# Low parts of weight blocks on VectorE, two blocks converted later, weight tiles in turned order, scaling on ScalarE: one change in four pieces

## The chip, the cores and the metric

The program runs on one core of one Trainium2 chip. The core has TensorE (matrix products, which only write the PSUM), VectorE, ScalarE and GpSimd (element by element; in the profile DVE, ACT and POOL) and SyncE (SP), which issues the DMAs here. Every engine runs its own list of instructions in order and waits at semaphores for the others. The metric is the time of one execution on the device in microseconds.

## The reference

Three parts follow each other, all in f32. The first is attention over 4 sequences of 576 tokens with 8 heads of 64 columns, with a mask by blocks of 64 tokens:

```python
scores = np.where(block_i >= block_j, scale * q @ k.T, -1e9)
attn = np.exp(scores - scores.max(-1)); attn /= attn.sum(-1) + 1e-9
x = attn @ v                                  # 2304 tokens x 512
h = x @ w_in                                  # 512 -> 2048
x = (h - np.tanh(h)) @ w_out                  # 2048 -> 512
xn = x / np.sqrt(np.mean(x * x, -1) + 1e-6) * rms_g
g = xn @ w_gate                               # 512 -> 1536
out = (g / (1 + np.exp(-g)) * (xn @ w_val)) @ w_out2
```

The five weight matrices arrive as 64-bit floats; the kernel turns their bits into f32 itself.

## The kernel before, in words

A product of two f32 matrices is made of three products with operands rounded to the shorter type f32r: each operand is split into a high part (`rnd`, line 100, mostly on ScalarE) and a low part, the difference between the full value and the high part (`lo`, line 105). So wherever TensorE needs a new operand, a rounding on ScalarE and a difference on VectorE or GpSimd come first. In the matmul lines 683 to 685, 873 to 875 and 961 to 963 the three belong together.

**First stage.** Tokens stand in 6 groups of 384. A step `s` is one of 16 blocks of 128 columns of the first feed-forward part in one group (`g, j = divmod(s, J1)`): 12 matmuls make `h`, ScalarE takes the tanh (line 881), VectorE the difference (line 887), ScalarE rounds it to `gh`, VectorE makes `gl`, and a step later 9 matmuls in `out1` add it into the sums of the group. Attention for the following groups is interleaved at slots of the step (`aslot`). In it `scores` takes the maximum on VectorE (line 479) and the exponential on ScalarE (line 481); after three tiles the reciprocal of the sums (line 490) and three scalings of the probabilities (line 494), which stood on GpSimd for the first two units and on VectorE for the later ones; `transp` turns the tiles on TensorE (line 507), and `av` multiplies by the values. The weights are converted in group 0, written to DRAM, and loaded again in every later group, two tiles of 512 KB in each step, into a ring of four (`w1get`).

**Blocks for the last part.** The last part uses a scheme with seven products instead of eight over pairs of token groups, so each of its 12 blocks of gate and value weights, and six of the output weights, becomes seven blocks of 256 columns. `Convert` does this: `load` (DMA), `piece` twice (lines 137 to 142 in `convert`), `sums` on GpSimd (four operations, lines 729 to 733), and the split into high part (ScalarE, line 738) and low part (line 739), in two halves of three and four column blocks. The list `away` does that in groups 2 to 4 for the output blocks and those gate blocks that are not in `DIRECT`, and writes them to DRAM. The blocks in `DIRECT` are made in place, in group 5 and while the first pair runs, and `keep` writes them out for the pairs behind.

**Last part.** For each of 3 pairs of groups `p` there are 12 steps `fast` of 42 matmuls (lines 961 to 963), with adds on VectorE (lines 1008 to 1018), Silu on ScalarE and a product on GpSimd (line 1017); behind them `tail` multiplies by the output weights, `sums(j)` (GpSimd, line 1024) having prepared further operands. Weights lie in three slots that `load_slot` fills two steps ahead.

TensorE's order is the order of the program text. The instructions of the other engines are put in order by a scheduler ahead of the run, except those in `pin`, which keep their order among themselves; so a change in one place can change the order of an engine elsewhere.

Of the kernel before, what the change touches and what calls it, by code (L numbers as in the profile page):

```python
# [10 lines left out]
F32 = mybir.dt.float32  # L11
# [40 lines left out]
DIRECT = (0, 1, 2, 3, 4, 6, 8)  # L52
# [39 lines left out]
def build(ctx, tc, q, k, v, w_in, w_out, w_gate, w_val, w_out2, rms_g, ident_in, out):  # L92
# [256 lines left out]
    class Attn:  # L349
# [107 lines left out]
        def scores(self, i, u, ti, d):  # L457
# [118 lines left out]
    with tc.manual_schedule(engines={PE.engine}):  # L576
# [20 lines left out]
        def jof(s):  # L597
            g, j = divmod(s, J1)
            return j
# [7 lines left out]
        def until(s):  # L607
            return s
# [102 lines left out]
        class Convert:  # L711
# [12 lines left out]
            def sums(self):  # L724

                f = self.f.rearrange("p g (k c) -> p (g k) c", k=2)
                o = self.o = env["cvp"].tile([128, 4, 256], F32, name="fs", tag="fs")
                gate = self.kind == "g"
                POOL.tensor_tensor(out=o[:, 0], in0=f[:, 3], in1=f[:, 2], op=ALU.add if gate else ALU.subtract)
                POOL.tensor_tensor(out=o[:, 2], in0=f[:, 1], in1=f[:, 3], op=ALU.subtract)  # L730
                x, y = (o[:, 0], f[:, 1]) if gate else (f[:, 1], o[:, 0])
                POOL.tensor_tensor(out=o[:, 1], in0=x, in1=y, op=ALU.subtract)
                POOL.tensor_tensor(out=o[:, 3], in0=f[:, 0], in1=o[:, 1], op=ALU.subtract)
# [7 lines left out]
            def split(self, w, eng):  # L741
                self.split_part(w[:, :, 0:3], eng, 0)
                self.split_part(w[:, :, 3:7], eng, 1)
                self.w = w

# [3 lines left out]
            def send(self, eng, half):  # L749
# [3 lines left out]
                self.split_part(w, eng, half)  # L753
# [6 lines left out]
        def away(units, eng):  # L760

            items = []
            for n, c in enumerate(units):
# [10 lines left out]
                def third(c=c):  # L774
                    c.sums()
                    c.send(eng, 0)
                items += [first, second, third, lambda c=c: c.send(eng, 1)]
# [42 lines left out]
        def slot(q):  # L820
# [4 lines left out]
                     + [Convert("g", j) for j in range(J2) if j not in DIRECT], POOL)  # L825
# [12 lines left out]
        for s in range(NSA):  # L838
# [61 lines left out]
            if 2 <= g < NG - 1:  # L900
                nit = {2: 0, 3: 10, 4: 26}[g] + (j + 1) * {2: 10, 3: 16, 4: 24}[g] // J1
                while 44 - len(items) < min(nit, 44):
                    items.pop(0)()
            if j == J1 - 1:
                while att.pos < goal:
                    att.step()
                if g == NG - 2:
# [20 lines left out]
                    items = away([direct[j] for j in DIRECT[:5]], POOL)  # L928
                    for n in range(3):
                        items[4 * n + 2] = direct[n].sums  # L930
                        items[4 * n + 3] = lambda n=n: direct[n].split(slot(n), POOL)
# [36 lines left out]
        BLOCK = {1: 2, 2: 0, 3: 1, 4: 6, 5: 3, 6: 4, 7: 5}  # L968

        KEEP = {0: 1, 1: 2, 2: 3, 3: 4, 5: 6, 7: 8}  # L970

        def load_slot(q):
# [4 lines left out]
            if j < J2:  # L977
                if p == 0 and j in direct:
                    direct[j].split(w, DVE)
# [6 lines left out]
        def temp(name, dt=F32):  # L986
            return w2b.tile([128, TG], dt, name=name, tag=name, bufs=2)
# [6 lines left out]
        def fast(s, j, x):  # L994
# [20 lines left out]
            DVE.tensor_tensor(c12, prod(6, xc, 1), c12, ALU.add)  # L1015
# [18 lines left out]
        def tail(p):  # L1034
# [19 lines left out]
            a = [temp(n)[:, 0:256] for n in ("c11", "c11", "c12")]  # L1054
# [71 lines left out]
        for p in range(NG // 2):  # L1126
            for j in range(J2):
# [4 lines left out]
                if p == 0:  # L1132
                    if j + 3 in direct:
                        if j + 3 >= 5:
                            direct[j + 3].piece(1)
                        direct[j + 3].sums()
# [34 lines left out]
```

## Time and profile before

| | |
|---|---|
| median of 3 runs | 1094.34 us (1094.28 to 1095.1) |
| the profiled execution | 1095.53 us, span 1093.7 us |
| TensorE busy | 1039.3 us, 95% of the span |
| VectorE busy | 844.5 us, 77% |
| ScalarE busy | 602.4 us, 55% |
| GpSimd busy | 442.6 us, 40% |
| granted clock of TensorE, mean | 0.981 |
| DMA | 291.74 MB, 267 GB/s |

The span runs from the first to the last instruction; the execution's own time has 1.8 us around it. A share over the whole span mixes stages, so the table by stages in the rows below is of more use. Group 2 begins near 250 us, group 5 near 580 us, the first pair of the last part at 674 us, its tail near 761 us.

### The profile page before, as it was taken

What the parts mean: (1) busy time and instruction counts of PE and PEld (TensorE: products, weight loads), DVE (VectorE), ACT (ScalarE), POOL (GpSimd) and SP (SyncE); (2) the same over time, 40 slices, a digit from 0 to 9 for tenths busy, and PEclk for the clock granted to TensorE, in tenths of its full rate; (3) what the DMA queues carried; (4) which work ended last, traced back from release to release, by engine and by line L of the source; (5) the groups of instructions that cost most, each with busy time, mean ns of one, the idle gap of its engine ahead of it and who ended that gap; (6) DMA issues with size and microseconds to landing.
All of it is one profiled execution on the core that took longest, in us unless ns stands there. A gap on an engine that the chain in (4) does not pass through costs nothing.

```text
span 1093.7 us, 18315 instructions
## 1 busy us (share of the span) xinstructions
PE 1039.3 (95%) x6020; PEld 943.4 (86%) x6020; DVE 844.5 (77%) x1714; ACT 602.4 (55%) x1390; POOL 442.6 (40%) x529
## 2 busy tenths in 40 slices
PE   7799999998899999999799899999999999999998
PEld 5566669997889988889688798999999998999998
DVE  5888867787878988888885677988886688866776
ACT  5877757667667776766665456442632226422253
POOL 5531111123434446445555564457421275212550
PEclk9999999999889999999999899999999999999999
DMA  9788888988779999997878996986687665786664
GB/s 224 231 282 293 271 282 269 275 237 247 201 185 255 263 330 290 319 298 244 282 253 299 371 355 215 391 311 253 238 282 286 252 246 198 277 296 248 233 224 162
DMA packets 192815, 291.74 MB, mean 267 GB/s; under 512 B 109776, under 2 KB 151120, under 8 KB 185424
## 3 DMA queue, kind: packets, MB, share of 16 engines
q1 hardware_dynamic: 192720, 290.57, 81.6%
q8 instruction: 48, 0.79, 0.3%
q14 instruction: 47, 0.39, 0.1%
HBM read 227.08 MB, written 63.44 MB: 266 GB/s over the span
## 4 chain that ended last, share of the span: by engine, by line
PE 71%; DVE 12%; ACT 6%; DMA 5%; issue 4%; POOL 1%; SPq 1%; DVEq 0%; ACTq 0%; POOLq 0%
PE gv L961 8%; PE gv L963 8%; PE gv L962 8%; PE gv L685 4%; PE t L873 4%; PE gv L684 4%; PE gv L683 4%; PE t L874 4%; PE t L875 4%; PE acc L685 3%; PE acc L683 3%; PE t L466 3%; PE acc L684 3%; PE acc L693 3%; PE t L560 2%
## 5 line engine op out<-in xcount | busy, mean ns | idle before, releaser
L961 PE MATMUL gv<-xh,ws 128*128 128x384 f32 x504 | 169.0, 335 | 1.0 <-DVE x2s L102 1.0
L963 PE MATMUL gv<-xh,ws 128*128 128x384 f32 x504 | 169.2, 336 | 0.0
L962 PE MATMUL gv<-xl,ws 128*128 128x384 f32 x504 | 169.0, 335 | 0.0
L873 PE MATMUL t<-xh,w 128*128 128x384 f32 x384 | 139.5, 363 | 0.1
L874 PE MATMUL t<-xl,w 128*128 128x384 f32 x384 | 130.6, 340 | 1.1 <-POOL xl L105 1.1
L875 PE MATMUL t<-xh,w 128*128 128x384 f32 x384 | 130.5, 340 | 0.0
L685 PE MATMUL acc<-w,gl 128*128 128x512 f32 x240 | 99.2, 413 | 12.8 <-DVE gl L105 12.8
L1017 POOL TENSOR_TENSOR g<-c,c 128x384 f32<-128x384 f32 x36 | 40.5, 1124 | 165.9 <-ACT c L1016 160.1
L683 PE MATMUL acc<-w,gh 128*128 128x512 f32 x240 | 101.3, 422 | 2.4 <-ACT gh L100 2.4
L481 ACT ACTIVATE pt<-pt,stat 128x64 f32<-128x64 f32 (+2 forms) x144 | 80.3, 559 | 42.0 <-DVE pt L479 41.2
L1014 ACT ACTIVATE gt<-c 128x384 f32<-128x384 f32 x36 | 18.9, 525 | 144.0 <-DVE c L1013 144.0
L684 PE MATMUL acc<-w,gh 128*128 128x512 f32 x240 | 97.1, 405 | 0.0
L961 PEld LDWEIGHTS gv<-xh,ws 128*128 128x128 f32 x504 | 94.6, 188 | 1.4 <-ACT sq L701 1.4
L963 PEld LDWEIGHTS gv<-xh,ws 128*128 128x128 f32 x504 | 94.6, 188 | 0.0
L962 PEld LDWEIGHTS gv<-xl,ws 128*128 128x128 f32 x504 | 94.6, 188 | 0.0
L873 PEld LDWEIGHTS t<-xh,w 128*128 128x128 f32 x384 | 73.5, 191 | 4.4 <-issue 0.7
L874 PEld LDWEIGHTS t<-xl,w 128*128 128x128 f32 x384 | 73.5, 191 | 3.5 <-POOL xl L105 1.4
L100 ACT ACTIVATE pp<-t 128x512 fp32r<-128x512 f32 (+6 forms) x152 | 64.1, 438 | 16.9 <-PE t L507 16.4
L479 DVE TENSOR_SCALAR_CACHE_REDUCE pt<-t 128x64 f32<-128x64 f32 (+2 forms) x144 | 63.7, 448 | 12.2 <-PE t L466 11.2
L875 PEld LDWEIGHTS t<-xh,w 128*128 128x128 f32 x384 | 72.9, 190 | 0.0
L105 DVE TENSOR_TENSOR gl<-gt,gh 128x384 fp32r<-128x384 f32 x80 | 60.8, 761 | 15.0 <-ACT gh L100 14.8
L887 DVE TENSOR_TENSOR gt<-t,gt 128x384 f32<-128x384 f32 x80 | 44.0, 550 | 35.6 <-ACT gt L881 35.5
(168 smaller groups left out, 2935.4 us busy)
## 6 DMA issues: line engine op xcount, KB each, us to landing
ws<-w2d SPq DMA_DIRECT2D x29, 1792.0 KB, 7.5
w<-w1d_i SPq DMA_DIRECT2D x80, 512.0 KB, 5.6
w<-w1d_o SPq DMA_DIRECT2D x64, 512.0 KB, 5.5
ws<-wod SPq DMA_DIRECT2D x21, 1536.0 KB, 6.1
st<-in_moe_w_out SPq DMA_DIRECT2D x28, 512.0 KB, 4.7
w2d<-ws SPq DMA_DIRECT2D x7, 1792.0 KB, 11.6
st<-in_moe_w_in SPq DMA_DIRECT2D x16, 512.0 KB, 5.4
w1d_i<-w SPq DMA_DIRECT2D x16, 512.0 KB, 4.6
```

What stands on the lines that cost most here:

```text
L100: ACT.activation(out=o, in_=i, func=AF.Copy)
L479: DVE.tensor_scalar(pt[:, a:z], s[:, 0:z - a], -0.125, least, ALU.mult, ALU.min, accum_out=mx)
L481: ACT.activation(out=pt[:, 0:keys], in_=pt[:, 0:keys], func=AF.Exp, scale=-1.0, bias=least, accum_out=st[:, 8 + ti:9 + ti])
L683: PE.matmul(acc, lhsT=gh[:, c], rhs=wh, start=first, stop=False)
L684: PE.matmul(acc, lhsT=gh[:, c], rhs=wl, start=False, stop=False)
L685: PE.matmul(acc, lhsT=gl[:, c], rhs=wh, start=False, stop=last)
L873: PE.matmul(h, lhsT=wh[:, c], rhs=xh[:, kk], start=(kk == 0), stop=False)
L874: PE.matmul(h, lhsT=wh[:, c], rhs=xl[:, kk], start=False, stop=False)
L875: PE.matmul(h, lhsT=wl[:, c], rhs=xh[:, kk], start=False, stop=(kk == KD - 1))
L961: PE.matmul(ps, lhsT=wh[:, c], rhs=xh[:, kk], start=(kk == 0), stop=False)
L962: PE.matmul(ps, lhsT=wh[:, c], rhs=xl[:, kk], start=False, stop=False)
L963: PE.matmul(ps, lhsT=wl[:, c], rhs=xh[:, kk], start=False, stop=(kk == nk - 1))
```

## The change

Four pieces. (1) The low parts of all converted blocks are made on VectorE instead of GpSimd; the four sums are now written over their inputs, so the first half is split before the sums and the second behind them (`fill`). The order of the seven products in `fast` follows, and two adds that read the same product become one of 768 columns. (2) Blocks 9 and 10 join `DIRECT`: they are no longer converted in groups 2 to 4, but while the first pair runs; their staging space is freed two steps later, so `sums` of the first pair start at step 9. (3) In groups 3 and 5 the weight tiles are taken from last to first, and the four that a group ends with are used by the next one without loading. (4) The scalings of the probabilities of the later units go from VectorE to ScalarE.

```diff
-DIRECT = (0, 1, 2, 3, 4, 6, 8)
+DIRECT = (0, 1, 2, 3, 4, 6, 8, 9, 10)
...
-                (POOL if u.light else DVE).tensor_scalar(pv, pv, st[:, 16 + t:17 + t], 1.0, ALU.mult, ALU.mult)
+                if u.light:
+                    POOL.tensor_scalar(pv, pv, st[:, 16 + t:17 + t], 1.0, ALU.mult, ALU.mult)
+                else:
+                    ACT.activation(out=pv, in_=pv, func=AF.Copy, scale=st[:, 16 + t:17 + t])
...
         def jof(s):
             g, j = divmod(s, J1)
-            return j
+            return J1 - 1 - j if back(g) else j
+
+        def back(g):
+            return g > 2 and g % 2 == 1
...
         def until(s):
-            return s
+            g, j = divmod(s, J1)
+            return s + 2 * (J1 - 1 - j) + 1 if 2 <= g < NG - 1 and j >= J1 - 4 else s
...
-                o = self.o = env["cvp"].tile([128, 4, 256], F32, name="fs", tag="fs")
...
-                POOL.tensor_tensor(out=o[:, 2], in0=f[:, 1], in1=f[:, 3], op=ALU.subtract)
+                POOL.tensor_tensor(out=f[:, 3], in0=f[:, 1], in1=f[:, 3], op=ALU.subtract)
...
-            def split_part(self, w, eng, half):
+            def split_part(self, w, half):
...
-                x = self.o if half else self.f.rearrange("p g (k c) -> p (g k) c", k=2)[:, 0:3]
+                x = self.f.rearrange("p g (k c) -> p (g k) c", k=2)[:, 0:4 if half else 3]
                 pin(ACT.activation(out=w[:, 0], in_=x, func=AF.Copy))
-                eng.tensor_tensor(out=w[:, 1], in0=x, in1=w[:, 0].bitcast(F32), op=ALU.subtract)
+                lo(DVE, w[:, 1], x, w[:, 0])
...
+            def fill(self, w, half):
                 self.w = w
+                self.split_part(w[:, :, 3:7] if half else w[:, :, 0:3], half)
+                if not half:
+                    self.sums()
...
-                nit = {2: 0, 3: 10, 4: 26}[g] + (j + 1) * {2: 10, 3: 16, 4: 24}[g] // J1
-                while 44 - len(items) < min(nit, 44):
+                nit = {2: 0, 3: 8, 4: 20}[g] + (j + 1) * {2: 8, 3: 12, 4: 20}[g] // J1
+                while 36 - len(items) < min(nit, 36):
...
-            DVE.tensor_tensor(c22, ps, c12, ALU.add)
-            DVE.tensor_tensor(c21, ps, c21, ALU.add)
+            ps = prod(6, xc, 0).rearrange("p (o c) -> p o c", o=1).broadcast_to([128, 2, TG])
+            DVE.tensor_tensor(vb, ps, va, ALU.add)
...
-                if p == 0 and j == JH:
+                if p == 0 and j == 8:
                     sw0.close()
                     sums_pool = sw.enter_context(tc.tile_pool(name="sums", bufs=1, side="right"))
-                if j > JH:
-                    if j == JH + 1:
-                        sums(0)
+                if j > 8:
+                    if j == 9:
+                        for k in range(3):
+                            sums(k)
                     sums(j - JH)
```

Line numbers move: the new lines 735 to 739 are the sums of a block (729 to 733 before), 744 its high part (738), 888 the tanh (881), 1019 to 1029 the adds and the last product of a step (1008 to 1019), 1027 GpSimd's product (1017), 1034 `sums` (1024), 801 and 803 the scaling and the differences of `xn` (794 and 796).

On GpSimd before, in the first pair, from the product of step 8 (`g1_8`) to that of step 10, each step's product is followed by three sums (`gs`) and then by the four differences of `xn`:

```order
L1017 TENSOR_TENSOR g1_8_8693<-c12_8638,c22_8640 128x384
L1024 TENSOR_TENSOR gs2_0_8705<-g1_2_8207,g1_8_8693 128x384
L1024 TENSOR_TENSOR g1_2_8207<-g0_2_8217,g1_2_8207 128x384
L1024 TENSOR_TENSOR gs2_1_8706<-gs2_0_8705,g0_2_8217 128x384
L1017 TENSOR_TENSOR g1_9_8768<-c12_8713,c22_8715 128x384
L1024 TENSOR_TENSOR gs3_0_8786<-g1_3_8290,g1_9_8768 128x384
L1024 TENSOR_TENSOR g1_3_8290<-g0_3_8300,g1_3_8290 128x384
L1024 TENSOR_TENSOR gs3_1_8787<-gs3_0_8786,g0_3_8300 128x384
L796 TENSOR_TENSOR xn_8543<-xn_8543 128x256 x4
L1017 TENSOR_TENSOR g1_10_8849<-c12_8794,c22_8796 128x384
```

On GpSimd now, the same place; `fu_8358` is block 10:

```order
L1027 TENSOR_TENSOR g1_8_8585<-va_8532,vb_8533 128x384
L735 TENSOR_TENSOR fu_8358<-fu_8358 128x256
L736 TENSOR_TENSOR fu_8358<-fu_8358 128x256
L1027 TENSOR_TENSOR g1_9_8659<-va_8606,vb_8607 128x384
L738 TENSOR_TENSOR fu_8358<-fu_8358 128x256
L739 TENSOR_TENSOR fu_8358<-fu_8358 128x256
L803 TENSOR_TENSOR xn_8432<-xn_8432 128x256 x4
L1034 TENSOR_TENSOR gs0_0_8677<-g1_0_7911,g1_6_8420 128x384
L1034 TENSOR_TENSOR gs1_0_8682<-g1_1_7987,g1_7_8506 128x384
L1034 TENSOR_TENSOR gs2_0_8687<-g1_2_8075,g1_8_8585 128x384
L1034 TENSOR_TENSOR gs3_0_8692<-g1_3_8151,g1_9_8659 128x384
L1034 TENSOR_TENSOR g1_0_7911<-g0_0_7921,g1_0_7911 128x384
```

The sums of block 10 stand on both sides of the product of step 9, and twelve `gs` sums (five are shown up to here) come in one run. They end with `gs3_1`, and the products of steps 10 and 11 follow, still on GpSimd now:

```order
L1034 TENSOR_TENSOR gs3_1_8693<-gs3_0_8692,g0_3_8161 128x384
L1027 TENSOR_TENSOR g1_10_8753<-va_8700,vb_8701 128x384
L803 TENSOR_TENSOR xn_8518<-xn_8518 128x256 x2
L1034 TENSOR_TENSOR gs4_0_8771<-g1_4_8238,g1_10_8753 128x384
L803 TENSOR_TENSOR xn_8518<-xn_8518 128x256
L1034 TENSOR_TENSOR g1_4_8238<-g0_4_8248,g1_4_8238 128x384
L1034 TENSOR_TENSOR gs4_1_8772<-gs4_0_8771,g0_4_8248 128x384
L1027 TENSOR_TENSOR g1_11_8832<-va_8779,vb_8780 128x384
```

The products of steps 10 and 11, which the tail reads, have moved behind the sums of the earlier steps. On VectorE now, between the last operations of step 9 and the first of step 10:

```order
L1028 TENSOR_TENSOR vb_8607<-gv_8661,vb_8607 128x384
L1029 TENSOR_TENSOR g0_9_8669<-vb_8607,gt_8608 128x384
L801 SCALAR_TENSOR_TENSOR xn_8432<-xn_8432,rinv_119,g_bc_7040 128x512
L801 SCALAR_TENSOR_TENSOR xn_8432<-xn_8432,rinv_119,g_bc_7040 128x2x256
L105 TENSOR_TENSOR gl_8878<-g1_9_8659,gh_8877 128x384
L105 TENSOR_TENSOR ws_8521<-fu_8358,ws_8521 128x1024
L1019 TENSOR_TENSOR va_8700<-gv_8711,c11_8699 128x384
```

The low part of block 10's second half (`ws`, 1024 columns) has come in between step 9's scaling of `xn` and step 10's first add; there was no such instruction here before. In the first stage, a unit of attention in group 3, VectorE before has the scalings between the low part of one step and the difference of the next:

```order
L105 TENSOR_TENSOR gl_4910<-gt_4906,gh_4909 128x384
L490 RECIPROCAL stat_4766<-stat_4766 128x3
L494 TENSOR_SCALAR pt_4767<-pt_4767,stat_4766 128x448
L494 TENSOR_SCALAR pt_4767<-pt_4767,stat_4766 128x512
L494 TENSOR_SCALAR pt_4767<-pt_4767,stat_4766 128x576
L140 TENSOR_SCALAR cv_4943<-cv_4943 128x512
L105 TENSOR_TENSOR pp_4892<-t_4965,pp_4892 128x8x64
L887 TENSOR_TENSOR gt_4978<-t_4958,gt_4978 128x384
```

ScalarE now has them (line 497) at this place, between the tanh and the rounding to `gh`:

```order
L489 ACTIVATE stat_4719<-stat_4719 128x3
L100 ACTIVATE pp_4851<-t_4922 128x8x64
L888 ACTIVATE gt_4935<-t_4915 128x384
L497 ACTIVATE pt_4720<-pt_4720,stat_4719 128x448
L497 ACTIVATE pt_4720<-pt_4720,stat_4719 128x512
L497 ACTIVATE pt_4720<-pt_4720,stat_4719 128x576
L100 ACTIVATE pp_4851<-t_4942 128x8x64
L100 ACTIVATE pp_4851<-t_4949 128x2x64
L100 ACTIVATE gh_4938<-gt_4935 128x384
```

The three scalings stand between the same step's tanh (`gt_4935`) and rounding (`gh_4938`) and moved from one engine's list to the other's.

## Rows read from the trace of the kernel before

**Rows 1.** Busy time by stages: start:end, us, engines, clock, DMA share, GB/s.

```profile
250.00:350.00 100.00, 90.56 (x496) 82.47 (x495) 81.14 (x207) 69.20 (x184) 38.71 (x55) 0.91 0.78 219
350.00:455.00 105.00, 100.23 (x545) 89.19 (x543) 91.47 (x192) 72.92 (x166) 50.19 (x57) 1.00 1.01 291
455.00:580.00 125.00, 115.96 (x619) 103.93 (x620) 97.71 (x192) 83.21 (x181) 65.77 (x74) 0.96 0.87 280
580.00:674.00 94.00, 87.30 (x437) 76.84 (x435) 64.34 (x93) 51.95 (x98) 53.26 (x46) 0.96 0.85 301
674.00:761.00 87.00, 86.55 (x496) 86.58 (x497) 74.28 (x124) 35.75 (x65) 46.05 (x45) 1.00 0.89 335
761.00:808.00 47.00, 44.57 (x369) 44.01 (x369) 41.65 (x70) 25.77 (x54) 23.35 (x23) 1.00 0.66 239
```

**Rows 2.** TensorE's waits, 170 to 690 us: waiter, releaser, us, times, longest.

```profile
PE acc L685 <- DVE gl L105: 12.8, 10, 3.4
...
PE t L531 <- DVE pp L105: 2.7, 3, 1.2
PE acc L683 <- ACT gh L100: 2.4, 1, 2.4
PE t L466 <- DVE avt L534: 2.1, 1, 2.1
PE t L507 <- DVE pt L479: 2.0, 1, 2.0
```

**Rows 3.** VectorE's timeline near 427 and 600 us: start, duration, instruction, idle before.

```profile
427.34 2.85 DVE L141 SCALAR_TENSOR_TENSOR cv<-cv,cu 128x512 int32<-128x512 int32 x1
...
597.78 2.23 DVE L140 TENSOR_SCALAR cv<-cv 128x512 f32<-128x512 f32 x1 [2.13 <-ACT cv L137]
600.12 0.69 DVE L141 SCALAR_TENSOR_TENSOR cv<-cv,cu 128x512 int32<-128x512 int32 x1
600.73 0.42 DVE L140 TENSOR_SCALAR cv<-cv 128x512 f32<-128x512 f32 x1
```

**Rows 4.** GpSimd's timeline at the same two places.

```profile
427.27 2.37 POOL L739 TENSOR_TENSOR wc<-fs,wc 128x1024 fp32r<-128x1024 f32 x1 [1.89 <-ACT wc L738]
...
597.33 2.41 POOL L739 TENSOR_TENSOR wc<-fs,wc 128x1024 fp32r<-128x1024 f32 x1 [5.27 <-ACT wc L738]
```

**Rows 5.** TensorE's timeline behind the first of them.

```profile
430.71 0.50 PE L685 MATMUL acc<-w,gl 128*128 128x512 f32 x1 [2.29 <-DVE gl L105]
```

**Rows 6.** Groups by line and form, low parts: count, busy us, mean ns, idle before.

```profile
L739 POOL TENSOR_TENSOR wc<-fs,wc 128x1024 fp32r<-128x1024 f32 x11 | 26.5, 2413 | 15.4 <-ACT wc L738 12.8 <-issue 1.8 <-POOL xs L535 0.7
...
L739 DVE TENSOR_TENSOR ws<-fs,ws 128x1024 fp32r<-128x1024 f32 x4 | 4.9, 1222 | 1.8 <-ACT ws L738 1.8
```

**Rows 7.** Groups by line: the scalings on VectorE, the exponentials on ScalarE.

```profile
L494 DVE TENSOR_SCALAR pt<-pt,stat 128x64 f32<-128x64 f32 (+5 forms) x96 | 40.8, 480 | 0.2
...
L481 ACT ACTIVATE pt<-pt,stat 128x64 f32<-128x64 f32 (+2 forms) x144 | 80.3, 559 | 42.0 <-DVE pt L479 41.2
```

**Rows 8.** Groups by line and form, operations of the last part.

```profile
L1012 DVE TENSOR_TENSOR c<-gv,c 128x384 f32<-128x384 f32 x36 | 19.7, 548 | 0.0
...
L794 DVE SCALAR_TENSOR_TENSOR xn<-xn,rinv,g_bc 128x512 f32<-128x512 f32 x18 | 19.7, 1133 | 0.0
...
L1016 ACT ACTIVATE c<-c 128x384 f32<-128x384 f32 x36 | 18.9, 525 | 14.1 <-DVE c L1015 14.1
...
L738 ACT ACTIVATE ws<-fs 128x1024 fp32r<-128x1024 f32 x7 | 7.4, 1059 | 6.8 <-POOL fs L733 6.7
...
L1017 POOL TENSOR_TENSOR g<-c,c 128x384 f32<-128x384 f32 x36 | 40.5, 1124 | 165.9 <-ACT c L1016 160.1 <-DMA st<-in_moe_w_val 5.8
...
L796 POOL TENSOR_TENSOR xn<-xn 128x256 f32<-128x256 f32 x36 | 31.7, 899 | 31.2 <-DVE xn L794 30.5
...
L1024 POOL TENSOR_TENSOR gs<-g,g 128x384 f32<-128x384 f32 x18 | 21.8, 1211 | 1.4
...
L733 POOL TENSOR_TENSOR fs<-fu,fs 128x256 f32<-128x256 f32 x18 | 14.5, 803 | 0.8
```

More of the change, by code (lines that the diff above doesn't have):

```diff
@@ L733, in sums @@
-                POOL.tensor_tensor(out=o[:, 3], in0=f[:, 0], in1=o[:, 1], op=ALU.subtract)
-            def split_part(self, w, eng, half):
-                x = self.o if half else self.f.rearrange("p g (k c) -> p (g k) c", k=2)[:, 0:3]
+                POOL.tensor_tensor(out=f[:, 2], in0=f[:, 3], in1=f[:, 2], op=ALU.add if gate else ALU.subtract)
+                POOL.tensor_tensor(out=f[:, 3], in0=f[:, 1], in1=f[:, 3], op=ALU.subtract)
+                x, y = (f[:, 2], f[:, 1]) if gate else (f[:, 1], f[:, 2])
@@ L738, in split_part @@
+                POOL.tensor_tensor(out=f[:, 1], in0=x, in1=y, op=ALU.subtract)
+                POOL.tensor_tensor(out=f[:, 0], in0=f[:, 0], in1=f[:, 1], op=ALU.subtract)
+            def split_part(self, w, half):
+                x = self.f.rearrange("p g (k c) -> p (g k) c", k=2)[:, 0:4 if half else 3]
                 pin(ACT.activation(out=w[:, 0], in_=x, func=AF.Copy))
-                eng.tensor_tensor(out=w[:, 1], in0=x, in1=w[:, 0].bitcast(F32), op=ALU.subtract)
-            def split(self, w, eng):
-                self.split_part(w[:, :, 0:3], eng, 0)
-                self.split_part(w[:, :, 3:7], eng, 1)
+                lo(DVE, w[:, 1], x, w[:, 0])
@@ L774, in third @@
                 def third(c=c):
+                    c.send(0)
                     c.sums()
-                    c.send(eng, 0)
-                items += [first, second, third, lambda c=c: c.send(eng, 1)]
+                items += [first, second, third, lambda c=c: c.send(1)]
             return items
@@ L824, in build @@
         items = away([Convert("o", j) for j in range(JH)]
-                     + [Convert("g", j) for j in range(J2) if j not in DIRECT], POOL)
+                     + [Convert("g", j) for j in range(J2) if j not in DIRECT])
         x = None
@@ L927, in build @@
                     direct = {j: Convert("g", j) for j in DIRECT}
-                    items = away([direct[j] for j in DIRECT[:5]], POOL)
+                    items = away([direct[j] for j in DIRECT[:5]])
                     for n in range(3):
-                        items[4 * n + 2] = direct[n].sums
-                        items[4 * n + 3] = lambda n=n: direct[n].split(slot(n), POOL)
+                        items[4 * n + 2] = lambda n=n: direct[n].fill(slot(n), 0)
+                        items[4 * n + 3] = lambda n=n: direct[n].fill(slots[n], 1)
                     items[14:16] = []
@@ L978, in load_slot @@
                 if p == 0 and j in direct:
-                    direct[j].split(w, DVE)
+                    direct[j].fill(w, 0)
+                    direct[j].fill(w, 1)
                     return
@@ L984, in load_slot, with temp @@
                 SP.dma_start(out=o.bitcast(F32), in_=wod[:, BLOCK[ORDER[j - J2]] ])
-        def temp(name, dt=F32):
-            return w2b.tile([128, TG], dt, name=name, tag=name, bufs=2)
+        def temp(name, k, dt=F32):
+            return w2b.tile([128, k, TG], dt, name=name, tag=name, bufs=2)
         def result(n, j):
@@ L1045, in split @@
                 f = left[i](j)
-                gh, gl = ([wk.tile([128, TG], F32R, name=n, tag=n) for n in ("gh", "gl")] if m % 2 else
-                          [temp(n, F32R) for n in ("c21", "c22")])
+                if m % 2:
+                    gh, gl = (wk.tile([128, TG], F32R, name=n, tag=n) for n in ("gh", "gl"))
+                else:
+                    both = temp("va", 2, F32R)
+                    gh, gl = (both[:, n] for n in range(2))
                 rnd(ACT, gh, f)
@@ L1132, in build @@
                 if p == 0:
[L1133 to L1136, printed above, removed]
+                    if j + 3 in DIRECT[5:]:
+                        direct[j + 3].piece(1)
                     if j + 4 in DIRECT[5:]:
```

27 lines of the change are left out of this document (13 added, 14 removed).

## The prediction

> **What bounds the kernel now.** I read the table by stages first [rows 1]. TensorE decides: in the first pair of the last part (674 to 761 us) it is busy for 86.55 of 87 us, while in the four stretches from 250 to 674 us, where attention and the first feed-forward part run together, it stands idle for 9.4, 4.8, 9.0 and 6.7 us, 30.0 in all. The same rows show a second loss: the granted clock averages 0.91, 0.96 and 0.96 in three of them (partly the 1.2 GHz level instead of 2.4 GHz), which is 9.0 + 5.0 + 3.8 = 17.8 us of full speed. The stretch with little idle time in one piece has 1.00, so the clock follows the stalls; 17.8 / 30.0 gives 0.59 us of clock per idle us.
>
> Next, TensorE's waits [rows 2]: 12.8 us for `gl`, the low part of the activations, which VectorE makes, and 9.2 us in the four other rows shown, 22.0 together. Then I followed them back. At 427.34 an integer step of a weight conversion (L141) takes 2.85 us on VectorE, at 597.78 a clamp (L140) 2.23; the same operations take 0.69 and 0.42 at 600.12 and 600.73 [rows 3]. In both cases GpSimd had just begun L739, the low part of a converted block, 2.37 and 2.41 us long, and VectorE comes free as that ends [rows 4]. The `gl` behind the first lets TensorE stand for 2.29 us [rows 5]. So the stalls are mostly not VectorE's load but an operation on GpSimd that holds it up.
>
> **The change part by part.** *Low parts to VectorE.* Between 250 and 674 us, 11 blocks of two halves leave GpSimd's L739 (the large half 2.41 us), and so do three more in the last stretch. VectorE takes over 9 + 3 blocks; its price for the large half is in the trace, 1.22 us [rows 6], which I use for both halves: 12 x 2.44 = 29 us of VectorE. *Scaling of probabilities.* 96 instructions leave VectorE, 40.8 us of its time [rows 7]. On ScalarE they cost between VectorE's own 0.48 us each and the 0.559 us of the exponentials of such tiles [rows 7]: 46 to 54 us; I take 50, midway, since both rows are of the same tiles. *Two blocks fewer converted early* takes about 4 x 1.8 us of pieces from VectorE (0.42 and 0.69 in rows 3, and a second integer step of some 0.69). VectorE's balance in this stage is 29 - 41 - 7 = -19 us, of 335 busy in 424 [rows 1]; ScalarE goes from 277 to at most 331. Neither is full.
>
> A rule speaks against this part. What the rows show is that two operations of VectorE, one with a single operand in the SBUF (L140) and one with two (L141), are held until GpSimd's ends [rows 3, 4]. The Trainium skill, page "SBUF — State Buffer", section "Who interferes with whom", puts it as an exclusive lock between the two engines, taken by a VectorE instruction with two inputs in the SBUF as well, whoever comes second being blocked for all of the first's instruction. The trace agrees (2.85 against 0.69 us). By that rule the low parts, which read two operands in the SBUF, go on being held by what GpSimd still does; the sum of this stage would then be rival C's and not the one below.
>
> What goes: of the 22.0 us of waits in rows 2 I take 20, since of the 16 waits behind them nearly all that I followed back lead to L739, alone or with a scaling that it held; lower end 10 (only the waits in whose chain nothing but L739 is late), upper end 22. With them goes their share of the clock, 20 x 0.59 = 12 us, lower end 6, upper end 17.8. What comes: ScalarE now has three scalings in a row, 3 x 0.56 = 1.7 us, ahead of `gh`, the rounding from which VectorE makes `gl`; the order shows it. There are 32 such triples. No row shows one there, so the bounds are nothing and half a triple each (a `gh` that becomes due somewhere in it waits half of it on average), 32 x 0.84 = 27 us. I take 7, nearer to the lower end, since a triple of 3 x 0.48 = 1.4 us stood in front of `gl` on VectorE before, and ScalarE is idle for a third of the stage. Sum for this stage: -20 - 12 + 7 = -25 us.
>
> *Order of weight tiles in groups 3 and 5.* It spares up to 12 pairs of loads. TensorE's waits in rows 2 name no DMA, so I price it at nothing; the cover is that tiles are asked for two steps ahead. If that cover were thin now, it could only gain.
>
> *Two more blocks in the first pair.* Here the order speaks. A step of this stage has 42 matmuls, at 86.55/496 = 0.1745 us [rows 1] 7.3 us, seven products of 1.05. Block 10 is split in two halves with GpSimd's sums between, and GpSimd has the product of step 9 (`g1_9`) in the middle of these sums. That product needs the sixth of step 9's seven products. From its end: add 0.55, Silu 0.53, product 1.12, two sums 2 x 0.80, ScalarE 1.06, VectorE 1.22 [rows 6, 8] = 6.1 us; TensorE has two products (2.1) to do meanwhile, so it stands 4.0 us. By VectorE's queue, from the end of the seventh product: add 0.55, a multiply between that and 1.13, two scalings of `xn` 2 x 1.13, a low part 0.55, the block's low part 1.22: 5.1 to 5.7, of which one product (1.05) is covered: 4.1 to 4.7. I take 4.3. Block 9 comes through the same queue: VectorE was busy 74.3 of 87 us here and gets two conversions of 2 x 1.8 + 2.44 = 6.0 more, less 12 x 0.15 by the merged add, so 84.5 of 87. Its stall lies between 0 and 4; I take 2.
>
> Then the tail. GpSimd now does twelve sums in one run before the product of step 10, and more before that of step 11. From the end of block 10's sums: four `xn` 3.6, twelve sums 12 x 1.21 = 14.5, product 1.1, three `xn` and three sums 6.3, product 1.1 = 26.6; then ScalarE and VectorE split it, 0.53 + 0.55: 27.7. TensorE in the same time: 2.3 until block 10's second half is there, six products 6.3, step 11 7.3, and five of the tail's first row of weight blocks, each 9 matmuls of 44.57/369 = 0.121 us [rows 1], 5.4: 21.3. It stands 6.4 us for that last operand, and the 2.4 us that it stands at this place now [rows 1] are part of it: 4.0 net. If the sums keep no faster than 1.21, this can grow to 6; if the step 10 stall is longer, it shrinks, as GpSimd catches up. Net idle 2 + 4.3 + 4.0 = 10.3, and by 0.59 per us 6 us of clock, of which I take 4, because GpSimd and VectorE catch up while TensorE is slow. Sum for the first pair +14; ends +5 (block 9 free, no clock lost, the tail 1) and +22 (4 + 4.7 + 6 and 7 of clock).
>
> In pairs two and three one add of 768 columns replaces two, some 0.15 us of VectorE a step beside a TensorE that is 100% busy: nothing.
>
> **Sum.** -25 + 14 = -11 on the profiled execution's 1095.5 us (span 1093.7 and 1.8 around it), so 1084.5; the median of the runs is 1.2 us below that execution, so I forecast **1083**.
>
> **Rivals.** *A: the first pair costs next to nothing*, since blocks 9 and 10 arrive earlier than the queues above suggest or TensorE's eight banks cover it. For it: at present the stage converts four blocks without a stall. Against it: a product of step 9 inside block 10's sums cannot be passed. It leaves +3: 1095.5 - 25 + 3 - 1.2 = 1072.
>
> *B: ScalarE takes VectorE's place, and the kernel gets slower.* One mechanism: a triple of scalings waits in ScalarE's queue for VectorE's reciprocal and holds up `gh`. The price is the time that each of the 32 holds TensorE, x: the forecast has x = 0.22. Each further us costs 1.3 with half of its clock, so from 11/1.3 = 8.5 us more, x = 0.48, nothing is gained; at x = 0.65 the stage gains 25 - 1.3 x 14 = 7 against 14: 1095.5 + 7 - 1.2 = 1101. For it: ScalarE's load rises from 65% to as much as 78%. Against it: only one wait in rows 2 is for ScalarE's `gh`.
>
> *C: the change doesn't do what it says: the low parts don't get rid of the hold.* They read two operands in the SBUF, and GpSimd keeps its sums and the low parts of `kl`, `vp`. Rows 3 and 4 show both kinds of operation held until GpSimd's ends; against it, the sums that remain on GpSimd are 0.8 us long [rows 8] instead of 2.4. Were half of the stalls to stay, the stage would gain (20 + 12)/2 - 4 = 12 (some triples would then wait behind stalls that are there anyway) and the first pair take it back: 1095.5 - 12 + 14 - 1.2 = 1096; with the first pair at its lower end 1087. It is the case of the lock in the Trainium skill, "SBUF — State Buffer", section "Who interferes with whom".
>
> **How the numbers follow.** Chances: forecast 0.52 (its own range 1074 to 1092: 9 us either way, since the ends of the terms don't fall together), A 0.17, B 0.18, C 0.13. A measurement of this kernel tells 0.2% (2.2 us) from no change. Faster: 0.50 of the forecast's 0.52 and A's 0.17, little of C: 0.68. Same: 0.02 of the forecast and half of C, 0.09. Slower: B and the rest of C, 0.23. The range that leaves out the best part of A and the worst of B is 1067 to 1101.
>
> **What the changed profile would show.** Right: no GpSimd operation over 1.7 us between 250 and 674 us; L140 and L141 near 0.42 and 0.69; TensorE's idle time there about 15 us instead of 30, its clock above 0.97 in all four stretches; a wait of 4 to 5 us in the second product of step 10 and one of about 6 us for a split operand at the tail's start. Wrong: if TensorE's largest waits there are for ScalarE's `gh` (B), if VectorE's operations are still at 1 us and more (C), or if the first pair stays dense (A).

## The result, and the profile after

Three runs of the changed kernel took 1079.0, 1080.7 and 1084.4 us, against 1093.8 to 1095.1 us before; a fourth, left out of every figure here, took 2590.3 us at a granted clock of 1.00, and nothing on record says why. The ratio is 0.9881, with a 95% interval of 0.9849 to 0.9913. 1083 us was forecast. The profiled execution took 1080.69 us, with a span of 1078.6 us.

The stages of the changed kernel, groups 2 to 5, the twelve steps of the first pair, its tail, and last a part of the pair (columns as in [rows 1]):

```profile
253.10:375.10 122.00, 116.74 (x662) 105.50 (x661) 93.42 (x235) 103.42 (x272) 43.60 (x65) 0.97 0.76 206
375.10:469.10 94.00, 90.11 (x479) 80.90 (x478) 69.34 (x139) 68.37 (x150) 32.78 (x46) 0.98 0.91 263
469.10:575.90 106.80, 100.62 (x560) 90.65 (x559) 82.68 (x164) 83.96 (x179) 45.15 (x61) 1.00 0.77 255
575.90:648.71 72.81, 71.55 (x376) 64.00 (x374) 58.12 (x91) 44.60 (x86) 22.07 (x24) 1.00 0.85 305
648.71:748.38 99.67, 91.64 (x505) 90.04 (x505) 84.31 (x124) 40.93 (x71) 50.08 (x52) 0.97 0.77 287
748.38:800.56 52.18, 50.60 (x422) 50.02 (x422) 44.77 (x78) 28.12 (x59) 25.09 (x24) 1.00 0.73 256
725.00:750.00 25.00, 18.68 (x90) 17.51 (x89) 18.33 (x24) 5.72 (x10) 24.76 (x25) 0.86 0.68 274
```

The first stage ends at 648.71 instead of 674.45 us: 25.7 us gained. The first pair's twelve steps take 99.67 instead of 87.95 us: 11.7 lost. The tail and all that follows are together 1.0 us shorter. In groups 2 to 5 TensorE stands idle for 5.3 + 3.9 + 6.2 + 1.3 = 16.7 us; between the same points of the program before it was 30.4. The granted clock is 0.97 or more in all four.

TensorE's waits, 170 to 690 us, beside [rows 2]:

```profile
PE acc L692 <- DVE gl L105: 3.3, 5, 1.1
PE acc L690 <- ACT gh L100: 3.0, 3, 1.7
PE t L534 <- DVE pp L105: 2.1, 3, 1.1
PE t L466 <- DVE avt L537: 1.7, 1, 1.7
PE t L466 <- DVE gt L894: 1.5, 2, 1.4
PE t L510 <- DVE pt L479: 1.5, 1, 1.5
```

The wait for `gl` falls from 12.8 to 3.3 us. That for ScalarE's `gh`, on which rival B rested, goes only from 2.4 to 3.0. The five kinds of wait shown in [rows 2] (the lines have moved) together fall from 22.0 to 11.6 us. GpSimd's longest kind of operation between 250 and 650 us is now the low part of `vp`:

```profile
L105 POOL TENSOR_TENSOR vp<-vr,vp 128x640 fp32r<-128x640 f32 x14 | 22.0, 1570 | 45.6 <-ACT vp L100 44.6 <-DMA qr<-in_q 0.9
```

TensorE's timeline in steps 9 and 10 of the first pair, each row the first matmul after a wait:

```profile
716.82 0.44 PE L968 MATMUL gv<-xh,ws 128*128 128x384 f32 x1 [0.94 <-ACT ws L744]
...
718.95 0.44 PE L970 MATMUL gv<-xh,ws 128*128 128x384 f32 x1 [1.51 <-DVE ws L105]
...
730.89 0.49 PE L968 MATMUL gv<-xh,ws 128*128 128x384 f32 x1 [4.71 <-ACT ws L744]
...
732.58 0.69 PE L970 MATMUL gv<-xh,ws 128*128 128x384 f32 x1 [0.87 <-DVE ws L105]
```

The waits are 0.94 + 1.51 = 2.45 us in step 9 and 4.71 + 0.87 = 5.58 in step 10. The two steps last 10.31 and 16.09 us instead of 7.32. In step 10 that leaves 8.77 - 5.58 = 3.2 us beyond the waits, mostly slow clock: 0.86 in the window from 725 us, where the product after the wait takes 1.92 instead of 1.05 us. The 0.5 us beyond the waits in step 9 is not, since the granted clock is 1.00 from 714.8 to 725.2 us. GpSimd, ScalarE and VectorE there:

```profile
718.79 1.31 POOL L1027 TENSOR_TENSOR g<-va,vb 128x384 f32<-128x384 f32 x1 [3.11 <-ACT va L1026]
724.66 0.74 POOL L735 TENSOR_TENSOR fu<-fu 128x256 f32<-128x256 f32 x1 [4.56 <-DVE ws L105]
725.48 0.74 POOL L736 TENSOR_TENSOR fu<-fu 128x256 f32<-128x256 f32 x1
726.21 1.28 POOL L1027 TENSOR_TENSOR g<-va,vb 128x384 f32<-128x384 f32 x1
727.45 1.17 POOL L738 TENSOR_TENSOR fu<-fu 128x256 f32<-128x256 f32 x1
728.70 1.05 POOL L739 TENSOR_TENSOR fu<-fu 128x256 f32<-128x256 f32 x1
```

```profile
722.22 0.85 ACT L744 ACTIVATE ws<-fu 128x768 fp32r<-128x768 f32 x1 [3.13 <-DVE fu L142]
...
729.78 1.06 ACT L744 ACTIVATE ws<-fu 128x1024 fp32r<-128x1024 f32 x1 [1.74 <-POOL fu L739]
```

```profile
717.68 1.21 DVE L105 TENSOR_TENSOR ws<-fu,ws 128x1024 fp32r<-128x1024 f32 x1
...
721.51 0.68 DVE L142 SCALAR_TENSOR_TENSOR fu<-st,cv 128x512 int32<-128x512 int32 x1
...
723.63 0.95 DVE L105 TENSOR_TENSOR ws<-fu,ws 128x768 fp32r<-128x768 f32 x1
```

The product of step 9 stands inside block 10's sums, as the order had shown, and costs them 1.2 us. But the sums themselves begin late, 5.9 us after the start of the product of step 8: ScalarE waited 3.13 us for the last piece (L142) of block 10, which stands on VectorE behind the low part of block 9's second half (717.68), and the sums wait for the low part of block 10's first half (723.63).

### The profile page after: what moved, and what is told of

It is laid out like the page before. It is cut to its first block, busy times and chain, and to the rows that moved or that the text cites. A ratio compares the mean times of both kernels' runs of the same rounds, so it can differ in the third digit from the quotient of the medians.

```text
span 1078.6 us, 18088 instructions
## 1 busy us (share of the span) xinstructions
PE 1031.9 (96%) x6020; PEld 937.0 (87%) x6020; DVE 815.0 (76%) x1610; ACT 643.9 (60%) x1486; POOL 384.7 (36%) x501
## 4 chain that ended last, share of the span: by engine, by line
PE 68%; DVE 13%; ACT 8%; DMA 4%; issue 4%; POOL 1%; SPq 1%; DVEq 0%; ACTq 0%; POOLq 0%
PE gv L970 6%; PE gv L968 6%; PE gv L969 6%; PE t L880 4%; PE t L882 4%; PE t L881 4%; PE gv L692 4%; PE gv L691 4%; PE gv L690 4%; PE acc L692 4%; PE acc L690 4%; PE acc L691 3%; PE t L466 3%; PE acc L700 3%; PE t L510 2%
## 5 line engine op out<-in xcount | busy, mean ns | idle before, releaser
L1027 POOL TENSOR_TENSOR g<-va,vb 128x384 f32<-128x384 f32 x36 | 39.0, 1083 | 189.4 <-ACT va L1026 189.4
L690 PE MATMUL acc<-w,gh 128*128 128x512 f32 x240 | 99.4, 414 | 3.6 <-ACT gh L100 3.0
L692 PE MATMUL acc<-w,gl 128*128 128x512 f32 x240 | 96.3, 401 | 3.3 <-DVE gl L105 3.3
L691 PE MATMUL acc<-w,gh 128*128 128x512 f32 x240 | 95.1, 396 | 0.0
L880 PEld LDWEIGHTS t<-xh,w 128*128 128x128 f32 x384 | 72.2, 188 | 3.5 <-issue 0.7
L882 PEld LDWEIGHTS t<-xh,w 128*128 128x128 f32 x384 | 72.0, 188 | 0.0
L510 PE MATMUL t<-ident,pt 128*128 128x128 f32 x400 | 65.8, 273 | 5.2 <-POOL pt L495 3.7
L105 POOL TENSOR_TENSOR vp<-vr,vp 128x640 fp32r<-128x640 f32 (+1 forms) x24 | 34.3, 1431 | 101.3 <-ACT vp L100 85.4
```

The source lines that it names most:

```text
L510: PE.transpose(t[:, (j - a) * 128:(j - a + 1) * 128], pt[:, j * 128:(j + 1) * 128], ident)
L690: PE.matmul(acc, lhsT=gh[:, c], rhs=wh, start=first, stop=False)
L691: PE.matmul(acc, lhsT=gh[:, c], rhs=wl, start=False, stop=False)
L692: PE.matmul(acc, lhsT=gl[:, c], rhs=wh, start=False, stop=last)
L880: PE.matmul(h, lhsT=wh[:, c], rhs=xh[:, kk], start=(kk == 0), stop=False)
L882: PE.matmul(h, lhsT=wl[:, c], rhs=xh[:, kk], start=False, stop=(kk == KD - 1))
```

## The experiments

Theory H: long operations on GpSimd hold VectorE up, and TensorE's stalls follow. Rival L: VectorE's plain load makes them. For the first pair, the question was what of the 11.7 us each late block costs. "First stage ends" is the start of the first pair in the profiled run; two profiles of the changed kernel differ there by 4.4 us, so a few us of it mean nothing. "Twelve steps" runs from the first to the last matmul of the steps, 0.2 us less than up to the tail as above. Each ratio is to the kernel before as run beside it, with medians of 1096.2 us for e1 to e3 and e5, 1097.4 for after_again, e4 and e7, and 1096.1 for e8 to e11; so compare ratios, and medians only within such a set. The 1.8 us more of e3_short's steps are all in its first step.

| run | ratio to before, 95% interval | median, us | first stage ends | twelve steps |
|---|---|---|---|---|
| before | 1 | 1094.3 | 674.5 | 87.8 |
| changed | 0.9881, 0.9849 to 0.9913 | (three runs above) | 648.7 | 99.5 |
| after_again | 0.9857, 0.9829 to 0.9886 | 1080.8 | 653.1 | 99.3 |
| e1_low | 0.9835, 0.9811 to 0.9859 | 1077.1 | 653.8 | 87.8 |
| e2_scale | 0.9973, 0.9953 to 0.9993 | 1094.4 | 673.2 | 87.8 |
| e3_short | 0.9952, 0.9935 to 0.9970 | 1092.1 | 668.5 | 89.6 |
| e5_order | 0.9880, 0.9858 to 0.9903 | 1083.7 | 646.9 | 98.8 |
| e4_early | 0.9837, 0.9810 to 0.9864 | 1078.8 | 656.1 | 87.8 |
| e7_mid | 0.9862, 0.9836 to 0.9887 | 1081.7 | 661.0 | 87.8 |
| e11_nine | 0.9898, 0.9877 to 0.9920 | 1084.7 | 654.8 | 90.0 |
| e9_low_scale | 0.9869, 0.9846 to 0.9891 | 1081.7 | 657.8 | 87.7 |
| e8_mid_order | 0.9769, 0.9744 to 0.9795 | 1070.3 | 651.3 | 87.7 |
| e10_kv | 0.9774, 0.9751 to 0.9797 | 1071.5 | 648.9 | 87.7 |

The changed kernel again, beside e4 and e7:

> The changed kernel itself, for the comparison on the same chip: ratio 0.985 to 0.991, the twelve steps of the first pair near 99.7 us.

It came out as expected.

**Low parts alone.**

```diff
-                eng.tensor_tensor(out=w[:, 1], in0=x, in1=w[:, 0].bitcast(F32), op=ALU.subtract)
+                lo(DVE, w[:, 1], x, w[:, 0])
```

> The kernel before, with the low parts of all converted blocks on VectorE and nothing else changed. Theory H (a long operation on GpSimd holds VectorE up): the first stage loses most of its waits for `gl`, groups 2 to 5 get 14 to 22 us shorter together, TensorE's first pair stays as it was, so 1073 to 1081 us. Rival L (VectorE's plain load makes the waits): VectorE takes over some 28 operations of 1.2 us without being relieved of anything, 34 us, so the waits for `gl` grow: 1096 to 1110 us. If the same hold remains under other names (GpSimd's sums and low parts of kl and vp): 1090 to 1096 us.

Measured: 1077.1 us, groups 2 to 5 shorter by 21.7 us. The stretch 250 to 640 us in one row each, the kernel before, then this one:

```profile
250.00:640.00 390.00, 361.77 (x1929) 324.44 (x1928) 308.68 (x642) 257.56 (x590) 189.25 (x216) 0.96 0.90 276
```

```profile
250.00:640.00 390.00, 372.96 (x2053) 336.56 (x2052) 324.81 (x691) 268.28 (x610) 149.09 (x200) 0.99 0.93 294
```

VectorE is busier, 324.8 instead of 308.7 us, and TensorE still gets 2053 matmuls done instead of 1929, with 17.0 instead of 28.2 us of idle time. By load it should have become slower. Rival L is refuted, and one piece gives as much as all four. That GpSimd's own results come too late, a rival not put on record, has little to stand on: of 30.5 us of TensorE's waits between 170 and 690 us before, 1.1 us are for GpSimd.

**Scaling alone.** The edit is the one of line 494 in the change.

> The kernel before, with the scalings of the later probabilities on ScalarE and nothing else changed. Theory H: L739 on GpSimd stays, and with it the waits; VectorE's 41 us are not what is short: 1090 to 1098 us. Rival L (VectorE's load makes the waits): 41 us less on VectorE are worth 10 us or more, 1076 to 1084 us. Rival B (a triple on ScalarE holds up `gh`): 32 triples at 0.2 to 0.65 us with half as much clock behind them, +8 to +27 us: 1102 to 1121 us.

```profile
250.00:640.00 390.00, 362.48 (x1944) 324.43 (x1943) 286.69 (x581) 291.27 (x660) 192.69 (x221) 0.96 0.90 280
```

VectorE is relieved of 22 us here, and TensorE's idle time stays at 27.5 us. Theory H again; a triple on ScalarE costs no measurable time either.

**Both together.**

> The kernel before with the low parts on VectorE and the scalings on ScalarE, without the late blocks and the turned order. Alone they gave ratios of 0.9835 and 0.9973. If they add up (VectorE now has the low parts and is relieved of 41 us elsewhere): 0.978 to 0.982, 1072 to 1077 us. If VectorE's load doesn't matter once nothing holds it up long: as the low parts alone, 1076 to 1081 us.

Neither: 0.9869 is no better than the low parts alone, and the intervals overlap. The scaling's 3 us don't add.

**Short instructions on GpSimd.**

```diff
+                for c in range(4 if half else 3):
+                    lo(POOL, w[:, 1, c], x[:, c], w[:, 0, c])
```

> The kernel before, with the low parts still on GpSimd, but one instruction for each column block of 256 (three or four in place of one of 768 or 1024; same data, same engine). It tells the length of one operation from the sum of GpSimd's work. Theory H, by length: an operation of VectorE waits at most for some 0.65 us instead of 2.4, so half or more of the gain of the low parts comes though no work has left GpSimd: 1076 to 1087 us. Rival S (what counts is how long GpSimd works in all): the sum is the same or a little larger by the fixed part of each instruction, 1093 to 1099 us.

A gain of 4 us, about a quarter of that of the low parts: nearer to rival S. In TensorE's waits `gl` fell only part of the way:

```profile
PE acc L685 <- DVE gl L105: 7.7, 8, 2.4
```

The other waits grew, and in the end TensorE's idle time in 250 to 640 us was 26.2 us. A sum over VectorE's operations from 175 to 690 us tells how much holding there is: of each that runs beside one of GpSimd, what it takes beyond the median of the same operation and shape with GpSimd idle. It is 59.8 us before, 53.9 here, 34.7 with the low parts moved, 29.8 in the changed kernel. Cutting the instruction makes more holds (79 of over 0.3 us instead of 69), not much less holding. So it is GpSimd's time on such operations that counts, more than the length of one. VectorE's and GpSimd's timelines of this run show the odd one:

```profile
523.43 4.44 DVE L140 TENSOR_SCALAR cv<-cv 128x512 f32<-128x512 f32 x1 [0.89 <-ACT cv L137]
```

```profile
523.25 2.83 POOL L105 TENSOR_TENSOR wc<-fs,wc 128x256 fp32r<-128x256 f32 x4
526.05 1.53 POOL L105 TENSOR_TENSOR vp<-vr,vp 128x640 fp32r<-128x640 f32 x1
```

A clamp of 0.42 us ends 0.29 us behind GpSimd's fifth operation in a row, so it seems held through all five.

**The hold by itself.** A kernel of its own starts one VectorE operation some 0.5 us after one on GpSimd:

```python
POOL.tensor_tensor(out=w[:, 1], in0=src, in1=w[:, 0].bitcast(F32), op=ALU.subtract)   # one of 1024, or 4 or 8 of 256
...
kind(o)                                            # clamp, shift, low part, scaling, add on VectorE
```

> The disputed cost by itself; nothing of the reference is computed. Five of VectorE's operations (the clamp L140 and the scaling L494 of 128x512 with one operand in the SBUF, the shift L141 of 128x512 and the low part `gl` of 128x384 with two, the add L1012 of 128x384 with one in the PSUM) start some 0.5 us after GpSimd has begun: nothing, one low part of 128x1024 (2.4 us), four of 128x256 (some 2.8 us in all), eight of 128x256 (5.6 us); three times each. Theory H1 (an operation is held until the GpSimd instruction that runs ends): the clamp takes about 2 us beside the one long instruction, at most 0.8 us beside the short ones. Theory H2 (it is held until a run of instructions on GpSimd ends, as one clamp of 4.44 us in the trace with short low parts suggests): 2 us, over 2 us, and about 5 us. The low part `gl` between 0.55 and 1.33 us, the add at 0.55 throughout; whether scaling and shift go with the clamp or with `gl` is open.

VectorE's rows of the clamp alone, beside one of 1024 columns and beside four of 256, then of the low part and of the add, alone and beside one of 1024:

```profile
12.19 0.43 DVE L60 TENSOR_SCALAR clamp<-f 128x512 f32<-128x512 f32 x1 [1.28 <-ACT f L80]
13.90 2.10 DVE L60 TENSOR_SCALAR clamp<-f 128x512 f32<-128x512 f32 x1 [1.28 <-ACT f L80]
...
24.04 0.48 DVE L60 TENSOR_SCALAR clamp<-f 128x512 f32<-128x512 f32 x1 [1.28 <-ACT f L80]
...
105.53 0.56 DVE L66 TENSOR_TENSOR low<-f,gh 128x384 fp32r<-128x384 f32 x1 [1.28 <-ACT f L80]
107.36 2.23 DVE L66 TENSOR_TENSOR low<-f,gh 128x384 fp32r<-128x384 f32 x1 [1.28 <-ACT f L80]
...
197.20 0.56 DVE L72 TENSOR_TENSOR add<-acc,f 128x384 f32<-128x384 f32 x1 [1.28 <-ACT f L80]
199.04 0.56 DVE L72 TENSOR_TENSOR add<-acc,f 128x384 f32<-128x384 f32 x1 [1.28 <-ACT f L80]
```

and GpSimd's beside the held clamp and the held low part:

```profile
13.37 2.34 POOL L82 TENSOR_TENSOR w<-src,w 128x1024 fp32r<-128x1024 f32 x1
...
106.84 2.34 POOL L82 TENSOR_TENSOR w<-src,w 128x1024 fp32r<-128x1024 f32 x1
```

The hold is real: 0.43 becomes 2.10, 0.56 becomes 2.23, and shift (0.69 to 2.36) and scaling (0.48 to 2.10) go alike. All end 0.3 to 0.5 us behind GpSimd's operation, that is, they run once it is done. Only the add with an operand in the PSUM is untouched. Beside short instructions VectorE gets in after the first (0.48): H1, not H2. I had put the low part at 1.33 at most, which was wrong. Why the clamp of 4.44 us was passed over four times, between the five operations, stays open.

**Plain order of tiles** (`jof` returns j, `until` returns s, as before):

> The changed kernel without the turned order of weight tiles in groups 3 and 5 (every group from first to last again, all tiles loaded). Theory: no wait of TensorE named a DMA, so the order is worth nothing: within 0.2% of the changed kernel, 1080 to 1085 us. Rival D (the 12 pairs of loads that are spared relieve the DMA queues, in group 5 above all, which got 10 us shorter): 1087 to 1092 us, with groups 3 and 5 longer and 2 and 4 as in the changed kernel.

The order is worth nothing here: 0.9880. No wait for a DMA came back.

**Which late block costs what.** Blocks 9 and 10 converted early again, or one of them, with the counts that hang on the list; e4_early also puts the start of `sums` back:

```diff
-DIRECT = (0, 1, 2, 3, 4, 6, 8, 9, 10)
+DIRECT = (0, 1, 2, 3, 4, 6, 8)        # e4_early; e7_mid: 8, 10; e11_nine: 8, 9
```

> The changed kernel with blocks 9 and 10 converted early again, as before (pieces 1, 3 and 4 of the change alone). The first pair's twelve steps took 11.7 us longer with the change. Theory (block 10's sums and the late low parts stall the first pair): 88 us again for the twelve steps, and the first stage gives back 1 to 4 us for the 8 more conversion items, so 1069 to 1077 us, ratio 0.975 to 0.983. Rival (the two blocks less are what relieves the first stage): the first stage goes back by 8 us or more, 1079 to 1084 us.

> The changed kernel with block 9 converted early again and block 10 left in the first pair. It parts the cost of the two blocks. Theory (block 10's sums with the product of step 9 between them stall step 10, 4 to 6 us with 3 to 4 us of clock; block 9 costs 2): the twelve steps take 95 to 98 us, 1079 to 1083 us. Rival (it is the number of blocks, that is VectorE's and GpSimd's load in the pair): half of the 11.7 us or more goes, the twelve steps take 88 to 93 us, 1073 to 1078 us.

> The changed kernel with block 10 converted early and block 9 late, so blocks 8 and 9 are converted for two steps in a row, and none after them. With block 10 alone late (8 and 10, a step between them) the twelve steps took 87.75 us and no step stalled. Theory R (what stalls is that blocks follow each other without a step between: the sums of the next come late and fall around a product): step 9 takes about 10.3 us as in the changed kernel, step 10 7.3, the twelve steps 90 to 92 us. Rival N (it takes all three): no step stalls, 88 us. Whole: 1076 to 1084 us, which tells less than the steps.

With both early the twelve steps are dense again, but the whole gains only 2 us on the changed kernel of the same chip (1078.8 against 1080.8), and the intervals overlap. Its profiled run is the fastest of six, so its 656.1 flatters it: by the medians the first stage gives back nearly all, the rival's case, and no run shows why. With block 10 alone late no step stalls, though it has the same sums, so the theory of e7_mid is refuted; its whole, 1081.7 us, is no faster than the changed kernel's either. In GpSimd's timeline of e7_mid:

```profile
723.62 1.02 POOL L1027 TENSOR_TENSOR g<-va,vb 128x384 f32<-128x384 f32 x1 [8.24 <-ACT va L1026]
726.47 0.73 POOL L735 TENSOR_TENSOR fu<-fu 128x256 f32<-128x256 f32 x1 [1.83 <-DVE ws L105]
...
729.22 1.16 POOL L739 TENSOR_TENSOR fu<-fu 128x256 f32<-128x256 f32 x1
730.34 1.01 POOL L1027 TENSOR_TENSOR g<-va,vb 128x384 f32<-128x384 f32 x1
```

The sums begin 2.85 us after the start of the product of step 8 instead of 5.87, and end as that of step 9 begins. With 8 and 9 in a row, step 9 takes 9.54 us and step 10 7.32: it is delayed by less than the 10.3 expected would give, and no product falls inside the sums. This fits that blocks stall when they follow each other without a step between, and that it adds up: 2.2 us of delay at the second in e11_nine (3.0 in the changed kernel), 8.8 at the third. Two limits: in the changed kernel the sums of blocks 3 and 4 follow each other as closely (658.83 and 666.16 us) and no step stalls, but their pieces were done on VectorE before the pair began; and block 9 without block 8 just ahead of it was not run, so the place in the pair is not told from the following.

**Two versions beyond the change.** The first takes e7_mid with the plain order. The second takes e4_early with:

```diff
-            lo(POOL, d["vp"][:, 0:nb, :, D:128], vr[:, 0:nb], d["vp"][:, 0:nb, :, 0:D])
+            lo(DVE, d["vp"][:, 0:nb, :, D:128], vr[:, 0:nb], d["vp"][:, 0:nb, :, 0:D])
...
-            lo(POOL, d["kl"][:, 0:W], d["kt"][:, 0:W], d["kh"][:, 0:W])
+            lo(DVE, d["kl"][:, 0:W], d["kt"][:, 0:W], d["kh"][:, 0:W])
```

> The changed kernel with block 9 converted early (block 10 late) and with the weight tiles in plain order, so pieces 1 and 4 and half of piece 2. Theory: the twelve steps of the first pair stay at 87.8 us as with block 9 alone taken back, and the order of tiles is worth nothing, so the first stage ends between 647 and 661 us, where these two edits put it one by one: 1070 to 1080 us. Rival: the first stage pays for each block that is converted early, and gives the 11 us back: 1080 to 1085 us.

> The changed kernel without the late blocks, and with the low parts of kl and vp (lines 320 and 337, GpSimd operations of 1.4 to 1.5 us, 34 between 250 and 690 us) on VectorE too: one step further on the way of the change. Theory H (GpSimd's longest operations hold VectorE up): what these hold up, 11 us of VectorE's time there, goes, and half of TensorE's 22 us of idle time in groups 2 to 5 with it: 1067 to 1075 us. Rival L (load): VectorE gets 34 operations of 0.7 to 0.9 us, 27 us, and is as full as before the change: 1080 to 1092 us.

Both beat the change by about 1%. The stretch 250 to 640 us of e4_early, then of e10_kv:

```profile
250.00:640.00 390.00, 369.00 (x2013) 332.01 (x2013) 305.92 (x626) 300.31 (x677) 147.19 (x203) 0.99 0.85 262
```

```profile
250.00:640.00 390.00, 373.17 (x2034) 335.51 (x2033) 315.95 (x664) 300.73 (x681) 105.32 (x170) 0.99 0.83 261
```

VectorE again takes on work (10 us more), GpSimd loses 42, and TensorE's idle time falls from 21.0 to 16.8 us. The sum of holds falls from 32.4 to 16.8 us. It is the second time that theory H gives the right sign against the load. For e8_mid_order the turned order alone separates it from e7_mid, and is worth 0.9% there, though nothing between the changed kernel and e5_order; TensorE's wait for `gl` is 7.9 us in the one and 3.6 in the other, and none names a DMA. Against e5_order, from which block 9 alone separates it, e8_mid_order gains 1.1%, about the 11 us by which its steps are shorter; in the turned order the same edit (e7_mid) gave nothing. Why is open: each edit, in all these runs, also gives the scheduler's lists another order. The two versions were not run together.

## Why the prediction was right, and where it was not

**The hold** (low parts away, L739 gone): right. e1_low shows that moving the low parts alone carries the gain, m_hold that the hold exists, and e2_scale that VectorE's load is not what was short. L140 and L141 came down less than I said, to means of 0.51 and 0.79 us (0.64 and 0.92 before): what GpSimd keeps goes on holding them.

**The first stage, -25**: measured -25.7, and -21.3 in the second profile. That the sum came out is partly luck: its two idle terms were both too big and cancelled. Idle time fell by 13.7 us, where -20 and +7 gave 13. But the +7, the price of triples on ScalarE, was hardly there (`gh` 2.4 to 3.0 us; e2_scale no slower), so the -20 was about -14. In the five kinds of wait from which I took it only 10.4 us went (22.0 to 11.6), the lower end of my range: that nearly all of them would go with L739 was wrong. [rows 2] leaves out another 8.5 us of waits, and the rest came from there. The clock gave some 11 us, busy time times what is missing to 1.00 (16.2 before, 5.3 after), where 12 was said.

**Rival C and the rule of the Trainium skill**, "SBUF — State Buffer", section "Who interferes with whom". m_hold agrees with the lock (2.10 against 0.43 us). The Trainium skill excepts, in that section, VectorE's operations with at most one operand in the SBUF, unless they run in a mode in which VectorE takes the shared ports for it ("2-port"). The same section of the Trainium skill counts `tensor_scalar` among those that can enter such a mode. m_hold agrees: the add is not held (0.56 both times), clamp and scaling, which are `tensor_scalar`, are; whether they run in such a mode no run shows. What I drew from it, half of the stalls staying, came nearer than my 20: of 59.8 us of holds 29.8 remain, and of 30.4 us of TensorE's idle time 16.7. The stage still gained 25, because the clock gave back 11 us instead of rival C's 6 and the triples cost hardly anything. In e10_kv the sum of holds falls to 16.8, and the time with it.

**The first pair, +14**: measured +11.7 in the steps and -0.5 in the tail. Block 9: 2 said, 2.45 measured. Block 10: 4.3 said, 5.58 measured, and here the step failed in its reason. I took the stall from the product of step 9 inside the sums, as if block 10 alone made it; e7_mid has block 10 alone and no stall. In the changed kernel block 10's first half is late, with block 9's low part ahead of it on VectorE. The clock, 4 said, took 3.2 at most.

**The tail, +4.0 net**: this term failed, a wait of 6.4 us for the operand made from the product of step 11. TensorE's only waits there:

```profile
749.60 0.39 PE L692 MATMUL gv<-ws,va 128*128 128x256 f32 x1 [0.74 <-DVE va L105]
...
752.84 0.39 PE L692 MATMUL gv<-ws,va 128*128 128x256 f32 x1 [0.84 <-DVE va L105]
```

1.58 us, less than the 2.4 before, and neither is for that operand: they stand at the first and third row of weight blocks, as the 2.4 before did, and it is the sixth. There GpSimd, VectorE and TensorE have:

```profile
753.62 1.01 POOL L1027 TENSOR_TENSOR g<-va,vb 128x384 f32<-128x384 f32 x1
```

```profile
755.22 0.89 DVE L105 TENSOR_TENSOR gl<-g,gh 128x384 fp32r<-128x384 f32 x1
```

```profile
756.32 0.28 PE L692 MATMUL gv<-ws,gl 128*128 128x256 f32 x1
```

Its low part is ready at 756.11 and is used at 756.32, without a wait. Both ends of the chain had moved. GpSimd's twelve sums took 12.9 us instead of 14.5 (the run from 733.87 to 746.72), so that the last product ends 24.9 us behind block 10's sums instead of 26.6. TensorE was slow in step 10 and waited once more: 18.6 us from these sums to the tail instead of 15.9; and its two waits in the tail come before this operand. I had seen that GpSimd catches up while TensorE is slow, and taken it off the clock only.

**The order of tiles, 0**: right for the change itself.

## What to carry to other kernels

When VectorE's durations swing between a short and a long value for the same shape, look at what GpSimd runs beside the long ones before counting VectorE's load: here a kernel that loaded VectorE more got 1.6% faster. Cutting such an operation in pieces is no substitute for taking it off GpSimd. And when late work comes in blocks, try a step between two of them: three in a row cost the steps 11 us here, two with a step between nothing. Then look at the whole: the same edit made the kernel 1.1% faster with one order of tiles and no faster with the other.

## What the hardware showed that I had not expected

A scaling with one operand and a scalar in the SBUF was held like operations with two (0.48 to 2.10 us), and the low part `gl` for the whole of GpSimd's operation. In e3_short one clamp seems to have waited through five GpSimd operations (4.44 us), while in m_hold VectorE got in after the first.
